# First steps of a two-transform and cosine-MLP kernel reordered: weight fold, cosine product and weight sums

## The chip, the cores and the metric

The kernel runs on one core of one Trainium2 chip. The metric is the device time of one execution in microseconds (us); lower is better. In the profile the engines are PE (TensorE; PEld is its weight load), DVE (VectorE), ACT (ScalarE), POOL (GpSimd) and SP (SyncE, which issues the DMAs).

## The reference

```python
X = np.fft.fft(x, axis=1)          # x: (8, 3008, 256) float32
X = np.fft.fft(X, axis=2)
a = X.real.reshape(8 * 3008, 256)
h = a @ w_in                       # w_in: (256, 2048)
g = h * np.cos(h)
out = g @ w_out                    # w_out: (2048, 256)
```

## The kernel before

The transform along the sequence is split 64 x 47. For each of the eight batches `first_half` does the part of length 47, its result goes through DRAM (`store_z`, `load_z`), and `second_half` does the part of length 64, group by group: six groups of token columns, 225 of them in group 0 and 256 in the others. It leaves a cosine part and a sine part per group in `pq`. The transform along the 256 channels is folded into the first weight matrix: `fold_weights(e, n)` multiplies a quarter n of `w_in` (512 columns) by the cosine (e = 0, into `WC`) or sine matrix (e = 1, into `WS`), and ACT copies the product out of PSUM. `take_wn(n)` then takes row 0 of that quarter of `WS` into the per-partition column `wn` with eight tiny matmuls and clears the row on GpSimd.

Because the output of a real transform has a mirrored half, one cosine product C and one sine product S give two token columns: C + S for a token and C - S for its mirror. That is one *half step* of the main loop, `k` = 0, 1, 2, ...; two half steps (u = 0, 1, two blocks of 128 hidden columns) are a *step* t = k // 2, and eight steps (fp = 0 to 7) finish one group of one batch. There are 384 steps. A half step h goes through:

- `seed` (ACT, L433): writes a start value into the PSUM tile `h.H`, a bank of four with tag "H";
- `mm1(h, 0)` (PE, L452, weights `WC`): adds the cosine product;
- `act_e` (ACT, L464): copies twice the cosine product to `ew`;
- `mm1(h, 1)` (PE, L452, weights `WS`): adds the sine product to the same bank, so it has to wait for `act_e`;
- `dve_h` (DVE, L468): `ew` minus `H`, the mirrored half;
- one half step later `act_round` (ACT, L480), `dve_frac` (DVE, L484) and `act_sin` (ACT, L490), which make the cosine;
- two half steps later `dve_g` (DVE, L494), the product h cos h;
- after both halves of a step `sums` (GpSimd, L510, L516, L517) makes four sums of the blocks;
- three steps later (`LAG`) `mm2` (PE, L543), the second matrix product. It works on seven products instead of eight: four with `g` blocks, of which the fourth needs the sums already, and three more with the sums. For the seven it needs sums of the output weights: `combine_w2(f0, f1)` (L418) makes them out of `w2` into `VX`, four instructions for two values of fp, each 128 x 256, reading `w2` with a step of two elements.

The schedule is written out by hand: instructions are queued per engine in the order of the program, each engine works its queue in order, and semaphores carry the dependencies. So what stands ahead of an instruction on its own engine decides as much as its data. In half step k the order around the change is: `mm1(k, 0)`, `act_e(k)`, `mm2` products 0 to 2 or 4 to 6, `dve_g(k-2)` (and `sums`), `act_round(k-1)`, `seed(k+1)`, `dve_frac(k-1)`, `act_sin(k-1)`, `mm1(k, 1)`, `mm2` product 3, `dve_h(k)`; then, after an odd k, the extra calls of the table `opening` for step t, and then those of `todo` (the next batch's transform).

Before the loop the first quarters are folded while the first x loads arrive; the last quarter's sine fold is queued in k = 0, its cosine fold and `take_wn(3)` after k = 1, and the four calls of `combine_w2` after t = 0, 1, 5 and 6, on DVE. `w2` comes in four DMAs of 512 KB: two issued at 35.9 to 36.9 us and two at 48.4 to 51.4 us.

Of the kernel before, what the change touches and what calls it, by code (L numbers as in the profile page):

```python
# [25 lines left out]
XP = 2 * IP  # L26
NG = 6
LAG = 3
SIN_SCALE = -float(np.float32(6.283185005187988))


# [50 lines left out]
def _width(g):  # L82
    return 225 if g == 0 else 256
# [24 lines left out]
def kernel(  # L108
# [7 lines left out]
    nc = tc.nc  # L116
# [78 lines left out]
    WC = cpool.tile([128, NDFF], FP, tag="WC", name="WC")  # L195
    WS = cpool.tile([128, NDFF], FP, tag="WS", name="WS")
# [4 lines left out]
    def psum(name, tag="H"):  # L201
        return ppool.tile([128, 512], FP, tag=tag, bufs=bank[tag], name=name)
# [85 lines left out]
    def second_half(b, g):  # L288

        T = _width(g)  # L290
        z2 = z2s[b]
        pb = psum("pb")
        for q in range(4):
            jj = 4 * g + q
            nc.tensor.matmul(  # L295
                pb[:, 128 * q : 128 * q + 128],
                lhsT=z2[:, jj * 128 : jj * 128 + 128],
                rhs=BJ[:, jj * 128 : jj * 128 + 128],
                start=q == 0,
                stop=True,  # L300
                skip_group_check=True,
            )
        pq = spool.tile([128, 512], FP, tag="pq", bufs=8, name="pq")
        pv = pq[:, 0 : 2 * T].rearrange("d (e t) -> d e t", e=2)
        bv = pb.rearrange("d (q e k) -> d e q k", q=4, e=2)
        if g == 0:
            nc.scalar.copy(
                out=pv[:, :, 0:192].rearrange("d e (q k) -> d e q k", k=64), in_=bv[:, :, 1:4, :]
            )
            nc.scalar.copy(out=pv[:, :, 192:225], in_=bv[:, :, 0, 0:33])  # L310
        else:
            nc.scalar.copy(out=pv.rearrange("d e (q k) -> d e q k", k=64), in_=bv)
        nb = spool.tile([128, 256], FP, tag="nb", bufs=8, name="nb")
        ready[b, g] = (pq, nb)
        if b == 0 and g == 0:
            return
        nd = dpool.tile([1, 256], FP, tag="nd", bufs=4, name="nd")
        nc.sync.dma_start(out=nd[:, 0:T], in_=pq[0:1, T : 2 * T])
        nc.sync.dma_start(out=nb[:, 0:T], in_=nd[0:1, 0:T].to_broadcast([128, T]))
# [9 lines left out]
    def transform(b):  # L329
        todo = {}  # L330

        def at(o, *call):
            todo.setdefault(o, []).append(call)

        for p in range(4):
            at(8 * p, load_x, b, p)
            for c, o, f in ((2 * p, 6, 9), (2 * p + 1, 9, 12)):
                at(8 * p + o, fold, b, c, 0)
                at(8 * p + o + 1, fold, b, c, 1)
                at(8 * p + f, first_half, b, c)  # L340
                at(8 * p + f + 1, store_z, b, c)
        at(23, load_z, b, 0)
        at(39, load_z, b, 1)
        for g in range(NG):
            at(42 + g, second_half, b, g)
        return todo
# [1 line left out]


    def fold_weights(e, n, tag="M"):  # L350
        W = WS if e else WC
        pw = psum("pw", tag)
        for i in range(2):
            nc.tensor.matmul(  # L354
                pw,
                lhsT=CS[i][:, 128 * e : 128 * e + 128],
                rhs=wr[n // 2][i][:, 512 * (n % 2) : 512 * (n % 2) + 512],
                start=(i == 0),
                stop=(i == 1),
            )  # L360
        nc.scalar.copy(out=W[:, 512 * n : 512 * n + 512], in_=pw)

    def take_wn(n):
        row = WS[0:1, 512 * n : 512 * n + 512]
        pw = psum("pw", "M")
        for k in range(4):
            nc.tensor.matmul(  # L367
                pw[:, k : k + 1],
                lhsT=row[:, 128 * k : 128 * k + 128],
                rhs=ones[:, 0:1],  # L370
                start=True,
                stop=True,
            )
        nc.scalar.copy(out=wn[:, 4 * n : 4 * n + 4], in_=pw[:, 0:4])
        if n == 0:
            nc.scalar.copy(out=wrow, in_=row[:, 0:256])
        nc.gpsimd.memset(row, 0.0)
# [15 lines left out]
    scratch = cpool.tile([1, 128], FP, tag="scratch", name="scratch")  # L393
    nc.scalar.activation(out=scratch, in_=ones, func=AF.Sin, bias=0.0, scale=SIN_SCALE / 8)

# [11 lines left out]
    vx = VX.rearrange("p (v f c) -> p v f c", v=4, c=128)  # L407
    wv = w2.rearrange("p (f u c j) -> p u j f c", u=2, j=2, c=128)

    def combine_w2(f0, f1):  # L410
        add, sub = ALU.add, ALU.subtract
        for dst, a, b, op in (
            (vx[:, 0], wv[:, 0, 1], wv[:, 0, 0], sub),
            (vx[:, 1], wv[:, 0, 1], wv[:, 1, 1], add),
            (vx[:, 2], vx[:, 0], wv[:, 1, 1], add),
            (vx[:, 3], wv[:, 1, 0], vx[:, 2], sub),
        ):
            nc.vector.tensor_tensor(  # L418
                out=dst[:, f0:f1], in0=a[:, f0:f1], in1=b[:, f0:f1], op=op
            )  # L420

# [15 lines left out]
    def seed_first(h):  # L437
        s, T = h.s, h.s.T
        nc.tensor.matmul(
            h.H[:, 0:T],  # L440
            lhsT=wrow[:, 128 * h.u : 128 * h.u + 128],
            rhs=s.pq[0:1, T : 2 * T],
            start=False,
            stop=True,
            skip_group_check=True,
        )

    def mm1(h, e):
        s, T = h.s, h.s.T
        W = WS if e else WC  # L450
        f = 2 * s.fp + h.u
        nc.tensor.matmul(  # L452
            h.H[:, 0:T],
            lhsT=W[:, 128 * f : 128 * f + 128],
            rhs=s.pq[:, e * T : e * T + T],
            start=False,
            stop=True,
            skip_group_check=True,
        )

    def act_e(h):
        T = h.s.T
        h.ew = spool.tile([128, 256], FP, tag="ew", bufs=2, name="ew")
        nc.scalar.mul(out=h.ew[:, 0:T], in_=h.H[:, 0:T], mul=2.0)  # L464
# [7 lines left out]
    def sides(h):  # L472
        T = h.s.T
        return h.s.r[:, 2 * T * h.u : 2 * T * h.u + 2 * T], h.H[:, 0 : 2 * T]
# [13 lines left out]
    def act_sin(h):  # L488
        r, _ = sides(h)
        nc.scalar.activation(out=r, in_=r, func=AF.Sin, bias=0.0, scale=SIN_SCALE)  # L490

# [216 lines left out]
    for half in range(2):  # L708
# [2 lines left out]
    load_w2(6, 8)  # L711
    load_bj(1024, NJ * 128)
    opening = {
        0: ((fold_weights, 0, 3), (take_wn, 3), (combine_w2, 0, 2)),
        1: ((combine_w2, 2, 4),),
        5: ((combine_w2, 4, 6), (second_half, 0, 1)),
        6: ((combine_w2, 6, 8),),
        10: ((second_half, 0, 2), (load_ident,)),
        14: ((second_half, 0, 3),),
        18: ((second_half, 0, 4),),  # L720
# [10 lines left out]
    n = len(steps)  # L731

    def step(t, last=None):
        s = steps[t] if 0 <= t < n else None
        return s if s is not None and (last is None or s.fp == 7) else None
# [3 lines left out]
    def unit(k):  # L739
        return halves[k] if 0 <= k < 2 * n else None  # L740
# [6 lines left out]
    steps[0].pq, steps[0].nb = ready[0, 0]  # L747
    for k in range(2 * (n + LAG)):
        t, u = divmod(k, 2)
        cur, prev, old, nxt = unit(k), unit(k - 1), unit(k - 2), unit(k + 1)  # L750
        done = step(t - LAG)
        full = step(t - LAG, True) if u else step(t - LAG - 1, True)
        if cur:
            if k % (2 * per) == 0:
                todo = transform(cur.s.b + 1) if cur.s.b + 1 < NB else {}
            mm1(cur, 0)
            if t == 0:
                seed_first(cur)
            act_e(cur)
            if k == 0:  # L760
                spread_nb()
                fold_weights(1, 3)
        if done:
            mm2(done, 4 * u, 4 * u + 3)
        if old:
            dve_g(old)
            if old.u:
                sums(old.s)
        if prev:
            act_round(prev)  # L770
        if nxt and k:
            seed(nxt)
        if full:
            take_m(full, 0 if u else 2, nc.scalar)
        if prev:
            dve_frac(prev)
            act_sin(prev)
        if cur:
            mm1(cur, 1)
        if done and u == 0:  # L780
            mm2(done, 3, 4)
        if cur:
            dve_h(cur)
        if full:
            take_m(full, 1 if u else 3, nc.vector)
        if u == 0:
            continue
        for i in range(6):
            s = step(t - LAG - 1 - i, True)
            if s:  # L790
                combine_m(s, i)
        for sg, lag in ((0, 5), (1, 7)):
            s = step(t - LAG - lag, True)
            if s:
                store_out(s, sg)
        for call in opening.pop(t, ()):
            call[0](*call[1:])
        for call in todo.pop(t % per, ()):
            call[0](*call[1:])
# [31 lines left out]
```

## Time and profile before

| | |
|---|---|
| time, median of 3 runs | 1979.02 us (1978.6 to 1979.23) |
| the profiled execution's own time | 1979.75 us |
| its span in the profile | 1977.9 us |
| PE, busy | 1960.2 us (99%) |
| DVE, ACT, POOL, busy | 1467.6 (74%), 1505.2 (76%), 1388.3 us (70%) |
| mean granted PE clock | 0.996 of full speed |
| first instruction of the main loop (`mm1(0, 0)`) | 38.6 us |

The profiled execution's time is 1.85 us longer than its span: what lies around the program's own instructions. All times below count from the start of the span. A PE row's duration holds the pipeline's fill; back to back, a product of `mm1` or `mm2` with 225 columns follows the one before after 0.38 us at the full clock and 0.75 us at half of it.

### The profile page before, as it was taken

Reading aid. Unit: us, or ns where it says so; the run is one execution under the profiler, and the core shown is the slowest. Engines: PE = TensorE matmul, PEld = TensorE weight load, DVE = VectorE, ACT = ScalarE, POOL = GpSimd, SP = SyncE. Lnnn points to the kernel's source line nnn. Section 1 sums busy time; section 2 is a strip of 40 time slices with the busy share of each in tenths; the row PEclk is TensorE's granted clock in tenths of the full one; section 3 lists DMA queues with packets and bytes.
Section 4 is the critical chain, followed back from the end, with each engine's and each line's share of the span. In section 5 each row is a group of like instructions: output and inputs, shape, how many; then the busy total and the mean of one; then the engine's idle time right before and its main releaser. Section 6 shows DMA issues by size and latency. Waiting matters only on the chain.

```text
span 1977.9 us, 29797 instructions
## 1 busy us (share of the span) xinstructions
PE 1960.2 (99%) x9360; PEld 1688.2 (85%) x9360; DVE 1467.6 (74%) x2540; ACT 1505.2 (76%) x3360; POOL 1388.3 (70%) x1577
## 2 busy tenths in 40 slices
PE   8899999999999999999999999999999999999998
PEld 4788889888998889888898888988889888898887
DVE  3777777777787777777777777777777777778776
ACT  3677778777787777777777777777777777778775
POOL 1577767777677776777667776687767777666775
PEclk9899999999999999999999999999999999999999
DMA  8422112120221212113121121113111231100001
GB/s 192 95 45 56 23 41 59 35 55 20 48 52 37 51 34 53 37 34 57 40 43 35 38 55 40 40 38 61 36 39 35 55 59 24 38 22 16 11 16 29
DMA packets 176691, 88.72 MB, mean 45 GB/s; under 512 B 103303, under 2 KB 173622, under 8 KB 174902
## 3 DMA queue, kind: packets, MB, share of 16 engines
q1 hardware_dynamic: 176374, 86.68, 21.2%
q8 instruction: 76, 1.25, 0.3%
q14 instruction: 81, 0.66, 0.1%
q10 hardware_dynamic: 160, 0.13, 0.0%
HBM read 49.50 MB, written 37.27 MB: 44 GB/s over the span
## 4 chain that ended last, share of the span: by engine, by line
PE 97%; DMA 1%; DVE 1%; SPq 0%; ACT 0%; issue 0%; POOL 0%; DVEq 0%; POOLq 0%
PE M L543 57%; PE H L452 33%; PE pz L242 3%; PE pb L295 2%; DMA xp<-in_x_dram 1%; DVE VX L418 0%; PE pw L354 0%; SPq L650 0%; DMA wr<-in_moe_w_in_dram 0%; DMA out_dram<-ob 0%; DVE r L484 0%; PE pd L399 0%; PE pw L367 0%; ACT ew L464 0%; ACT r L490 0%
## 5 line engine op out<-in xcount | busy, mean ns | idle before, releaser
L510 POOL TENSOR_TENSOR S<-r 128x512 f32<-128x512 f32 (+1 forms) x383 | 475.2, 1241 | 476.3 <-PE M L543 239.5
L484 DVE SCALAR_TENSOR_TENSOR r<-r,H 128x512 f32<-128x512 f32 (+1 forms) x768 | 518.9, 676 | 287.4 <-ACT r L480 273.5
L490 ACT ACTIVATE r<-r 128x512 f32<-128x512 f32 (+1 forms) x768 | 477.8, 622 | 277.2 <-DVE r L484 276.6
L543 PE MATMUL M<-S,VX 128*128 128x256 f32 (+1 forms) x2304 | 612.4, 375 | 0.0
L494 DVE SCALAR_TENSOR_TENSOR r<-H,r 128x512 f32<-128x512 f32 (+1 forms) x768 | 518.4, 675 | 99.7 <-ACT r L490 50.1
L543 PEld LDWEIGHTS M<-S,VX 128*128 128x128 f32 x2304 | 438.1, 190 | 50.3
L452 PE MATMUL H<-pq,WC 128*128 128x256 f32 (+1 forms) x1536 | 458.8, 380 | 0.4 <-ACT H L433 0.2
L452 PE MATMUL H<-pq,WS 128*128 128x256 f32 (+1 forms) x1536 | 452.8, 377 | 5.6 <-ACT ew L464 5.5
L480 ACT ACTIVATE r<-H 128x512 f32<-128x512 f32 (+1 forms) x768 | 447.7, 583 | 0.0
L468 DVE TENSOR_TENSOR H<-ew,H 128x256 f32<-128x256 f32 (+1 forms) x768 | 325.2, 423 | 95.4 <-PE H L452 22.1
L543 PE MATMUL M<-r,w 128*128 128x256 f32 (+1 forms) x1536 | 389.4, 376 | 0.0
L464 ACT ACTIVATE ew<-H 128x256 f32<-128x256 f32 (+1 forms) x768 | 290.3, 378 | 103.9 <-PE H L452 92.8
L433 ACT ACTIVATE H<-nb,wn 128x256 f32<-128x256 f32 (+1 forms) x766 | 366.0, 478 | 0.0
L452 PEld LDWEIGHTS H<-pq,WC 128*128 128x128 f32 x1536 | 280.1, 190 | 78.3 <-ACT r L490 43.6
L452 PEld LDWEIGHTS H<-pq,WS 128*128 128x128 f32 x1536 | 291.8, 190 | 40.2 <-ACT ew L464 8.6
L543 PEld LDWEIGHTS M<-r,w 128*128 128x128 f32 x1536 | 299.7, 197 | 29.4 <-ACT mr L566 1.2
L516 POOL TENSOR_TENSOR S<-S,r 128x256 f32<-128x256 f32 (+1 forms) x383 | 276.0, 721 | 30.0
L517 POOL TENSOR_TENSOR S<-r,S 128x256 f32<-128x256 f32 (+1 forms) x383 | 275.7, 720 | 30.0
L543 PE MATMUL M<-r,VX 128*128 128x256 f32 (+1 forms) x768 | 228.5, 379 | 0.2
L543 PE MATMUL M<-S,w 128*128 128x256 f32 (+1 forms) x768 | 225.2, 375 | 0.0
L543 PEld LDWEIGHTS M<-r,VX 128*128 128x128 f32 x768 | 143.3, 190 | 23.4 <-issue 7.6
L543 PEld LDWEIGHTS M<-S,w 128*128 128x128 f32 x768 | 150.5, 196 | 14.6
(67 smaller groups left out, 917.5 us busy)
## 6 DMA issues: line engine op xcount, KB each, us to landing
out_dram<-ob SPq DMA_DIRECT2D x728, 32.0 KB
xp<-in_x_dram SPq DMA_DIRECT2D x56, 256.0 KB
zd<-zs SPq DMA_DIRECT2D x112, 96.0 KB
z<-zd SPq DMA_DIRECT2D x28, 384.0 KB
xp<-in_x_dram SPq DMA_DIRECT2D x56, 120.0 KB
nb<-nd SPq DMA_DIRECT2D x40, 128.0 KB
wr<-in_moe_w_in_dram SPq DMA_DIRECT2D x8, 256.0 KB
w<-in_moe_w_out_dram SPq DMA_DIRECT2D x4, 512.0 KB
```

The source lines that it names most:

```text
L433: nc.scalar.activation(out=h.H[:, 0:T], in_=s.nb[:, 0:T], func=AF.Copy, bias=0.25, scale=wn[:, f : f + 1])
L452: nc.tensor.matmul(h.H[:, 0:T], lhsT=W[:, 128 * f : 128 * f + 128], rhs=s.pq[:, e * T : e * T + T], start=False, stop=True, skip_group_che ...
L464: nc.scalar.mul(out=h.ew[:, 0:T], in_=h.H[:, 0:T], mul=2.0)
L468: nc.vector.tensor_tensor(out=h.H[:, T : 2 * T][:, ::-1], in0=h.ew[:, 0:T], in1=h.H[:, 0:T], op=ALU.subtract)
L480: nc.scalar.activation(out=r, in_=y, func=AF.Copy, bias=BIG, scale=1.0)
L484: nc.vector.scalar_tensor_tensor(out=r, in0=r, scalar=-BIG, in1=y, op0=ALU.add, op1=ALU.subtract)
L490: nc.scalar.activation(out=r, in_=r, func=AF.Sin, bias=0.0, scale=SIN_SCALE)
L494: nc.vector.scalar_tensor_tensor(out=r, in0=y, scalar=-0.25, in1=r, op0=ALU.add, op1=ALU.mult)
L510: tt(out=sv[:, 0:2], in0=qv[:, 1:2].to_broadcast([128, 2, T]), in1=qv[:, 0:4:3], op=ALU.subtract,)
L516: tt(out=sv[:, 2], in0=sv[:, 1], in1=gv[:, 0, 0], op=ALU.subtract)
L517: tt(out=sv[:, 3], in0=gv[:, 1, 0], in1=sv[:, 2], op=ALU.add)
L543: nc.tensor.matmul(acc[key][m // 2][:, 256 * (m % 2) : 256 * (m % 2) + T], lhsT=w, rhs=a, start=first, stop=s.fp == 7, skip_group_check=True,)
```

## The change

Four things in the first twelve half steps:

- The first `second_half(0, 0)` takes its PSUM bank from the four with tag "M" instead of those with tag "H".
- The last quarter's cosine fold and `take_wn(3)` are cut in two. The matmuls of the fold go into k = 1 between `mm1(1, 0)` and `mm1(1, 1)`, those of `take_wn` into k = 2 between `mm1(2, 0)` and `mm1(2, 1)`; their copies on ACT follow `act_sin`.
- For half steps 3, 4 and 5 `mm1(h, 0)` and `act_e(h)` are queued one half step ahead: in half step h - 1, after `act_sin` and before `mm1(h - 1, 1)`.
- `combine_w2` runs on GpSimd instead of DVE. The calls for fp 0 to 3 both stand after t = 0, the other two are halved and stand after t = 3 and 4, and after t = 5 and 6.

```diff
+AHEAD = 2 * LAG
...
-        pb = psum("pb")
+        pb = psum("pb", "H" if b or g else "M")
...
     def fold_weights(e, n, tag="M"):
-        W = WS if e else WC
+        keep_weights(e, n, weights(e, n, tag))
+
+    def weights(e, n, tag="M"):
         pw = psum("pw", tag)
...
+        return pw
+
+    def keep_weights(e, n, pw):
+        W = WS if e else WC
         nc.scalar.copy(out=W[:, 512 * n : 512 * n + 512], in_=pw)
 
     def take_wn(n):
+        keep_wn(n, weight_row(n))
+
+    def weight_row(n):
         row = WS[0:1, 512 * n : 512 * n + 512]
         pw = psum("pw", "M")
...
+        return pw
+
+    def keep_wn(n, pw):
+        row = WS[0:1, 512 * n : 512 * n + 512]
         nc.scalar.copy(out=wn[:, 4 * n : 4 * n + 4], in_=pw[:, 0:4])
...
-    def combine_w2(f0, f1):
+    def combine_w2(f0, f1, k0=0, k1=4):
...
-        ):
-            nc.vector.tensor_tensor(
+        )[k0:k1]:
+            nc.gpsimd.tensor_tensor(
...
     opening = {
-        0: ((fold_weights, 0, 3), (take_wn, 3), (combine_w2, 0, 2)),
-        1: ((combine_w2, 2, 4),),
-        5: ((combine_w2, 4, 6), (second_half, 0, 1)),
-        6: ((combine_w2, 6, 8),),
+        0: ((combine_w2, 0, 2), (combine_w2, 2, 4)),
+        3: ((combine_w2, 4, 6, 0, 2),),
+        4: ((combine_w2, 4, 6, 2, 4),),
+        5: ((combine_w2, 6, 8, 0, 2), (second_half, 0, 1)),
+        6: ((combine_w2, 6, 8, 2, 4),),
...
-            mm1(cur, 0)
-            if t == 0:
-                seed_first(cur)
-            act_e(cur)
+            if k not in range(3, AHEAD):
+                mm1(cur, 0)
+                if t == 0:
+                    seed_first(cur)
+                act_e(cur)
             if k == 0:
                 spread_nb()
                 fold_weights(1, 3)
+            elif k == 1:
+                pw = weights(0, 3)
+            elif k == 2:
+                pw = weight_row(3)
...
             dve_frac(prev)
             act_sin(prev)
+        if k == 1:
+            keep_weights(0, 3, pw)
+        elif k == 2:
+            keep_wn(3, pw)
+        if k + 1 in range(3, AHEAD):
+            mm1(nxt, 0)
+            act_e(nxt)
         if cur:
             mm1(cur, 1)
```

## The prediction

> **What bounds the kernel now.** The page comes first.
>
> ```profile
> PE 1960.2 (99%) x9360; PEld 1688.2 (85%) x9360; DVE 1467.6 (74%) x2540; ACT 1505.2 (76%) x3360; POOL 1388.3 (70%) x1577
> ```
>
> PE is busy for all but 18 us, and from 88 us on every stretch I asked for is full. The change touches nothing behind half step 15, so it can win only what PE loses ahead of 88 us. The windows view, cut where the granted clock changes, shows where that is (window, PE, PEld, DVE, ACT, POOL busy, granted clock, DMA share, GB/s):
>
> ```profile
> 47.00:50.40 3.40, 2.29 (x9) 1.23 (x10) 1.62 (x4) 2.39 (x7) 0.52 (x1) 1.00 1.18 202
> 50.40:53.80 3.40, 2.95 (x7) 1.59 (x7) 3.31 (x7) 2.23 (x6) 2.51 (x3) 0.50 1.23 188
> 53.80:57.20 3.40, 1.81 (x5) 0.92 (x5) 2.89 (x7) 1.72 (x5) 0.75 (x1) 0.50 1.12 294
> 57.20:60.70 3.50, 3.50 (x11) 3.13 (x11) 1.62 (x3) 2.18 (x5) 1.65 (x3) 0.50 1.08 384
> 60.70:76.30 15.60, 15.60 (x85) 14.99 (x83) 12.34 (x24) 10.81 (x26) 7.27 (x9) 1.00 0.25 45
> 81.10:84.60 3.50, 1.35 (x6) 0.76 (x5) 3.10 (x7) 1.85 (x5) 0.79 (x1) 0.99 0.09 16
> 84.60:88.00 3.40, 3.40 (x10) 2.91 (x10) 1.31 (x3) 2.14 (x6) 2.83 (x4) 0.50 0.01 2
> ```
>
> There are two holes, 47 to 57 us and 81 to 84.6 us, and each brings a stretch at half clock (10.3 and 3.4 us) in which PE is full but slow. What made the holes is in the chain that ended last (start us, us, what):
>
> ```profile
> 49.88 0.25 ACT ew L464
> 50.13 0.44 ACT r L480
> 50.60 0.62 DVE r L484
> 51.23 0.31 DVE H L468
> 51.54 2.05 DVE VX L418 x3
> 53.61 0.43 DVE VX L418
> 54.04 0.54 DVE r L494
> ...
> 77.81 2.12 DVE VX L418 x3
> 79.96 1.37 DVE VX L418
> 81.33 0.54 DVE r L494
> ```
>
> The output weight sums (L418) stand in DVE's queue ahead of `dve_g` and `dve_frac`; `act_sin` waits for `dve_frac`, the next `act_e` stands behind `act_sin`, and `mm1(k, 1)` waits for `act_e`. The third look is DVE's and GpSimd's own timeline: one sum takes DVE 0.42 us where GpSimd is idle, but up to 1.37 us beside a GpSimd instruction.
>
> ```profile
> 46.25 0.42 DVE L418 TENSOR_TENSOR VX<-w,VX 128x256 f32<-128x256 f32 x1
> 79.61 1.44 POOL L218 TENSOR_TENSOR xf<-xp 94x508 f32<-94x508 f32 x1
> 79.96 1.37 DVE L418 TENSOR_TENSOR VX<-w,VX 128x256 f32<-128x256 f32 x1
> ```
>
> **What the holes cost.** Back to back, a product with 225 columns comes every 0.38 us at full clock (0.43 with 256). From `mm1(2, 0)` at 47.14 to `mm1(8, 0)` at 62.98 us lie 12 products of `mm1` and 10 of `mm2`, 22 x 0.38 = 8.4 us of work in 15.8. From `mm1(13, 0)` at 74.64 to `mm1(17, 0)` at 88.28 lie 20 products of 0.38 and two of 0.43, 8.5 us in 13.6. So 7.4 us are lost in the first hole, 5.2 in the second; the first can't vanish, since half steps 2 to 5 have no `mm2` beside them.
>
> **The sums on GpSimd.** 16 instructions leave DVE: 1.5 us at 45 us, 2.5 at 51.5, 2.4 at 72 and 3.5 at 77.7. On GpSimd the nearest row is L516, 128 x 256 out of SBUF: 0.73 us, one every 0.80. It has no operand with a step of two elements. From below the fold's subtraction (L218, one operand reversed, 94 x 508 in 1.26) gives 0.65 per 256 columns; from above 128 x 512 (1.28 us) stands for reading twice the words. I take 0.80, since the reversed operand costs nothing there. The first eight run as soon as `w2` lands: its 1 KB packets pass between 38 and 42 us, and the second half, issued from 48.4 us, between 53.8 and 57.5. So GpSimd, idle until 47.3 in the old trace, works on them from about 40.5 to 46.9. Queued behind them are the clearing of the `WS` row (0.52 us) and `sums(0)`, which can't start before about 49 anyway. The other eight go into steps 3 to 6, two in each: `sums` takes 2.65 us from start to free (1.14 + 2 x 0.75), plus 1.6, so 4.25 of a step of 11 x 0.38 = 4.2. In step 6 the next batch's fold (1.3) comes on top, and GpSimd falls 1.6 us behind. Who waits for that: `mm2` needs `sums` of a step about two steps after they can begin, 8.4 us less 1.1 for L510, so 7.3 us of cover; `VX` for fp 4 is ready about 66 us and used about 71. Cost: nothing. With p for one instruction, the cover goes in the opening at 40.5 + 8p + 1.1 = 56.4 (p = 1.85) and in steps 3 to 6 at 8p - 4.8 = 7.3 (p = 1.5).
>
> The Trainium skill speaks against this move (GPSIMD Engine Reference, section Engine selection): elementwise work belongs on VectorE, and two-input operations run about twice as slow on GpSimd. The trace agrees on the instruction alone, 0.73 against 0.42 us, but not for DVE's rows beside GpSimd, 0.65 to 1.37. By the rule 16 x 0.3 = 5 us would be lost if GpSimd's queue were on the path, which I deny.
>
> With DVE free, the second hole has no cause left: DVE has 0.54 + 0.39 + 0.54 = 1.5 us per half step, ACT's ring (below) 1.95, PE 2.1. **Gain 5.2 us**, its half clock included, since without a hole nothing lowers the clock.
>
> **Fold and row in the gaps.** In k = 1 the four fold passes (4 x 0.43, with their start 1.82) begin behind `seed_first` at 43.26 instead of 44.35, where PE used to wait 0.45 for `act_e`. `mm1(1, 1)` comes at 45.08 (before 43.87), `mm1(2, 0)` at 45.46 (before 47.14). The row's eight matmuls (0.95) follow until 46.85. On ACT the fold's copy (0.59) goes ahead of `act_e(2)`: 45.42, then 46.04. `seed(3)` at 46.72 no longer waits for `dve_g(0)`, because the first `pb` has left the H banks; that edit costs nothing and moves no DMA. SP's queue keeps its order.
>
> **The cosine product ahead.** Queued so, PE runs `mm1(k+1, 0)` before `mm1(k, 1)`, and `mm1(k+1, 0)` needs `seed(k+1)`, which on ACT stands behind `act_round(k-1)`. The ring from one `act_round` to the next is then: 0.43 to `seed`'s start, 0.50 for it, 0.38 for the first product, 0.69 until the second is out, 0.43 for `dve_h` and the handover, 2.43 us. The old order has two rings of 1.95: ACT's own (round 48.08, sin 49.31, next `act_e` 49.79, next round 50.03) and `act_e` to `act_e` over PE (47.82 to 49.79). So this part is slower by 0.48 per turn wherever nothing else interferes. Laid out with the old rows' durations: `act_round(2)` 48.71, `act_round(3)` 51.13, `act_round(4)` 53.55, `seed(6)` ends 54.44, `mm1(6, 0)` 54.48 (before 56.93). From there `mm2` fills PE: 11 products later `mm1(8, 0)` stands at 54.48 + 4.18 = 58.66 instead of 62.98. Gain 4.3 us at full clock.
>
> **The clock.** From 46.85 to 54.48 PE has 7 products, 2.7 us of work in 7.6, thinner than the window 47.0 to 50.4 after which the old trace falls to half clock. I therefore expect the fall at 50 to 52 us. A turn of the ring then takes 2.43 + 0.37 + 0.47 = 3.27; one to two turns are hit (1.05 on average), and the dense part begins about 55.5 at half clock. It returned, in both old cases, at the end of a full stretch of 3.4 us; so I count 2 to 4.4 us of dense work at half speed, of which half is lost, 1.6. First hole: 4.3 - 2.65 = **1.7 us**, between 0.5 and 4.3.
>
> The Trainium skill says the same of the gate (TensorE: Matmul & The Clock Gate, section What's actually happening): half rate after an idle window of about 3.4 us, full rate after a busy one. The rows 10.3 and 3.4 agree; how thin "idle" is they leave open, hence the next rival.
>
> **Sum.** 5.2 + 1.7 = 6.9 us: 1979.75 becomes 1972.85 for the profiled execution. The median lies 0.7 below that one, so 1972.1. A measurement of this kernel tells about 0.2%, 4 us, from no change: below 1975.1 counts as faster.
>
> **Rivals.**
>
> *The clock stays full.* If 35% of work is enough to hold it, both holes close as far as they can: 4.3 + 5.2 = 9.5 us, 1969.5. Against it: 47.0 to 50.4. Chance 0.12.
>
> *The second hole only moves.* If GpSimd's 1.6 us behind in step 6 reach PE after all (a late `xf`, S or `VX`), PE loses perhaps 2 us once and half of 3.4 at half clock, 3.7 of the 5.2: a gain of 3.2, 1975.8. Against it: 7.3 us of cover. Chance 0.14.
>
> *Slower: GpSimd reads the step of two badly.* It decides from p = 1.5 us and undoes the whole gain at p = 2.1 (8 x 0.6 = 4.8 in steps 3 to 6, 2.0 in the opening). At p = 2.5, twice the row of 128 x 512, the opening's sums end 5.2 us too late and the others 7.9 us: 13.1 against 6.9, 1985.3. For it: no row with that step on GpSimd. Against: the reversed operand is free. Chance 0.06.
>
> *The parts cancel.* The longer ring and three windows at half clock eat the first gain, and DVE's sums had hidden another wait of like size at 81 us: 1979. Against it: the chain names L418 directly. Chance 0.06.
>
> The forecast, the first hole at half clock and the second gone, keeps 0.62 (1971.4 to 1973.3).
>
> **How the numbers follow.** Faster: 0.62 + 0.12 + a part (0.05) of the second rival, 0.79. Same: 0.09 of it and 0.05 of the cancelling, 0.14. Slower: 0.07. The range takes in the full clock (1969.5, less 0.5 of spread between runs) and the moved hole: 1969.0 to 1976.0.
>
> **What would show it.** L418 on POOL at 0.7 to 0.8 us, the first eight over by 48 us; `mm1(2, 0)` about 45.5, `mm1(6, 0)` between 54.5 and 56; `act_round` to `act_round` 2.4 us or more for half steps 2 to 4; a clock of 0.5 from 50 to 52 us to 57 to 61; no PE gap over 0.5 us from there to 100 us. The prediction is wrong if L418 takes over 1.5 us, if PE waits on POOL, or if a hole is left at 70 to 85 us.

## The result and the profile after

The changed kernel took 1971.87 us (median of six runs, 1970.68 to 1973.18) against 1979.09 for the kernel before (six runs, 1978.60 to 1979.66): a ratio of 0.9963, 95% interval 0.9951 to 0.9976, so 7.2 us faster. The profiled execution took 1971.01 us with a span of 1969.2, 8.7 us shorter than before. L numbers of the changed kernel are its own: `combine_w2` is L432, `mm1` L466, `act_e` L478, `act_round` L494, `mm2` L557.

The page's busy times first:

```profile
PE 1954.4 (99%) x9360; PEld 1686.3 (86%) x9360; DVE 1458.7 (74%) x2524; ACT 1505.5 (76%) x3360; POOL 1398.8 (71%) x1593
```

16 instructions went from DVE to POOL, which is 10.5 us busier. PE's busy time fell by 5.8 us at the same number of products: it spent 10.2 us less at half clock (table below), and half of that, 5.1 us, is most of the fall. The windows view (window, PE, PEld, DVE, ACT, POOL busy, granted clock, DMA share, GB/s), cut at this run's clock changes:

```profile
46.80:50.20 3.40, 1.69 (x8) 0.99 (x6) 1.81 (x4) 2.54 (x7) 1.64 (x3) 1.00 1.17 201
50.20:53.60 3.40, 1.68 (x6) 0.98 (x6) 2.42 (x6) 2.50 (x6) 0.99 (x3) 1.00 1.22 190
53.60:57.00 3.40, 3.25 (x9) 2.94 (x10) 1.97 (x4) 2.40 (x6) 2.18 (x3) 0.50 1.15 346
57.00:60.50 3.50, 3.50 (x20) 3.44 (x19) 2.03 (x5) 1.84 (x5) 1.78 (x3) 1.00 1.00 308
60.50:76.30 15.80, 15.80 (x88) 15.51 (x87) 11.72 (x22) 12.40 (x30) 13.11 (x18) 1.00 0.45 76
76.30:80.00 3.70, 3.70 (x21) 3.49 (x20) 2.93 (x6) 3.05 (x9) 3.54 (x5) 1.00 0.42 65
80.00:88.00 8.00, 8.00 (x46) 6.70 (x45) 5.96 (x11) 6.07 (x14) 6.14 (x8) 1.00 0.01 2
```

The second hole is gone: PE is full from 57 us on. The first is still there, 47 to 53.6 us, with PE half empty, but only one stretch of 3.4 us at half clock follows. What fills it is no longer DVE's output weight sums; in the chain that ended last (start us, us, what) it is the ring over the seed (L447):

```profile
47.50 0.41 DVE H L482
47.91 0.02 issue
47.93 0.55 ACT r L494
48.48 0.35 ACT H L447
48.83 0.04 issue
48.87 1.04 PE H L466 x4
49.92 0.02 issue
49.94 0.41 DVE H L482
50.35 0.02 issue
50.37 0.55 ACT r L494
```

From one `act_round` to the next: 50.37 - 47.93 = 2.44 us. GpSimd's timeline shows the eight opening sums and how `sums(0)` (L524) follows without having waited for them. They start when the first half of `w2` is there: the first row waits for several semaphores, and the wait that this trace puts down to PE is put down to the DMA of `w2` in the run "sums twice".

```profile
40.52 1.42 POOL L432 TENSOR_TENSOR VX<-w 128x256 f32<-128x256 f32 x2 [5.65 <-PE pw L357]
41.89 0.73 POOL L432 TENSOR_TENSOR VX<-VX,w 128x256 f32<-128x256 f32 x1
...
45.58 0.74 POOL L432 TENSOR_TENSOR VX<-w,VX 128x256 f32<-128x256 f32 x1
46.31 0.52 POOL L391 MEMSET WS<- 1x512 f32 x1
48.51 1.07 POOL L524 TENSOR_TENSOR S<-r 128x450 f32<-128x450 f32 x1 [1.68 <-DVE r L508]
```

To compare runs, the starts of `mm1(k, 0)` on PE are counted from `mm1(0, 0)`; that one itself stood between 36.8 and 38.6 us in the runs, as the first loads came (38.57 before, 37.69 after; of this 0.9 us, 0.77 is the last x load in the chain, which ended at 26.67 us before and at 25.90 after, ahead of anything that the change touches). So 0.9 of the 8.7 us between the two spans is not counted as the change's.

| us after mm1(0, 0) | mm1(2, 0) | mm1(6, 0) | mm1(8, 0) | mm1(17, 0) | half clock, us | median, us |
|---|---|---|---|---|---|---|
| before | 8.57 | 18.36 | 24.41 | 49.71 | 10.24 + 3.41 | 1979.09 |
| changed | 6.98 | 16.06 | 21.95 | 42.09 | 3.41 | 1971.87 |
| changed, again | 6.98 | 16.06 | 21.73 | 41.87 | 3.41 | 1972.03 |
| sums only | 8.57 | 17.55 | 23.34 | 43.48 | 10.24 | 1971.14 |
| all but sums | 6.98 | 18.50 | 24.50 | 49.80 | 10.24 + 3.41 | 1978.80 |
| not ahead | 6.98 | 15.30 | 20.79 | 40.93 | 6.83 | 1969.38 |
| sums thrice | 6.97 | 17.38 | 25.48 | 50.54 | 10.24 + 3.41 | 1983.44 |
| sums twice | 6.98 | 17.74 | 23.48 | 43.63 | 10.24 | 1972.53 |
| fold back | 8.57 | 19.95 | 26.45 | 46.59 | 13.65 | 1974.93 |
| seed early | 6.98 | 14.48 | 18.73 | 38.81 | none | 1969.41 |
| PE filled | 6.98 | 16.16 | 20.35 | 40.49 | none | 1970.00 |
| seed early and filled | 6.98 | 14.48 | 18.73 | 38.80 | none | 1967.72 |
| not ahead and filled | 6.98 | 14.66 | 18.96 | 39.09 | none | 1968.03 |

The half-clock column counts the stretches before 100 us of the profiled execution, which is one run; the medians are of 5 to 11 runs. The kernel before ran at 1978.45, 1978.64 and 1978.74 us beside the three sets of experiments, so medians of different sets are best compared by what each gained on the kernel before beside it: the changed kernel 7.2 and, run again, 6.7 us.

### The profile page after: what moved, and what is told of

It reads as the page before. It is cut to its first block, busy times and chain, and to the rows that moved or that the text cites. A ratio compares the mean times of both kernels' runs of the same rounds, so it can differ in the third digit from the quotient of the medians.

```text
span 1969.2 us, 29797 instructions
## 1 busy us (share of the span) xinstructions
PE 1954.4 (99%) x9360; PEld 1686.3 (86%) x9360; DVE 1458.7 (74%) x2524; ACT 1505.5 (76%) x3360; POOL 1398.8 (71%) x1593
## 4 chain that ended last, share of the span: by engine, by line
PE 97%; DMA 1%; SPq 0%; ACT 0%; DVE 0%; issue 0%; POOL 0%; DVEq 0%; POOLq 0%
PE M L557 58%; PE H L466 34%; PE pz L243 3%; PE pb L296 2%; DMA xp<-in_x_dram 1%; PE pw L357 0%; SPq L664 0%; DMA wr<-in_moe_w_in_dram 0%; DMA out_dram<-ob 0%; PE pd L413 0%; ACT r L494 0%; ACT H L447 0%; DVE H L482 0%; PE H L453 0%; PE pw L377 0%
## 5 line engine op out<-in xcount | busy, mean ns | idle before, releaser
L524 POOL TENSOR_TENSOR S<-r 128x512 f32<-128x512 f32 (+1 forms) x383 | 475.1, 1240 | 463.5 <-PE M L557 237.7
L557 PE MATMUL M<-S,VX 128*128 128x256 f32 (+1 forms) x2304 | 612.4, 375 | 0.0
L557 PEld LDWEIGHTS M<-S,VX 128*128 128x128 f32 x2304 | 437.7, 190 | 50.1
L466 PE MATMUL H<-pq,WC 128*128 128x256 f32 (+1 forms) x1536 | 457.7, 380 | 3.7 <-ACT H L447 3.7
L466 PE MATMUL H<-pq,WS 128*128 128x256 f32 (+1 forms) x1536 | 450.2, 375 | 0.1
L494 ACT ACTIVATE r<-H 128x512 f32<-128x512 f32 (+1 forms) x768 | 447.7, 583 | 1.1 <-DVE H L482 1.1
L557 PE MATMUL M<-r,w 128*128 128x256 f32 (+1 forms) x1536 | 388.7, 375 | 0.0
L478 ACT ACTIVATE ew<-H 128x256 f32<-128x256 f32 (+1 forms) x768 | 290.4, 378 | 101.7 <-PE H L466 90.3
L447 ACT ACTIVATE H<-nb,wn 128x256 f32<-128x256 f32 (+1 forms) x766 | 366.0, 478 | 0.0
L466 PEld LDWEIGHTS H<-pq,WC 128*128 128x128 f32 x1536 | 279.8, 190 | 80.5 <-ACT r L504 43.6
L557 PEld LDWEIGHTS M<-r,w 128*128 128x128 f32 x1536 | 299.2, 197 | 29.3 <-ACT mr L580 1.2
L466 PEld LDWEIGHTS H<-pq,WS 128*128 128x128 f32 x1536 | 291.5, 190 | 32.6 <-issue 0.7
L557 PE MATMUL M<-r,VX 128*128 128x256 f32 (+1 forms) x768 | 228.1, 378 | 0.2
L557 PE MATMUL M<-S,w 128*128 128x256 f32 (+1 forms) x768 | 225.2, 375 | 0.0
L557 PEld LDWEIGHTS M<-r,VX 128*128 128x128 f32 x768 | 143.0, 190 | 23.4 <-issue 7.7
L557 PEld LDWEIGHTS M<-S,w 128*128 128x128 f32 x768 | 150.4, 196 | 14.6
```

The source lines that it names most:

```text
L447: nc.scalar.activation(out=h.H[:, 0:T], in_=s.nb[:, 0:T], func=AF.Copy, bias=0.25, scale=wn[:, f : f + 1])
L466: nc.tensor.matmul(h.H[:, 0:T], lhsT=W[:, 128 * f : 128 * f + 128], rhs=s.pq[:, e * T : e * T + T], start=False, stop=True, skip_group_che ...
L494: nc.scalar.activation(out=r, in_=y, func=AF.Copy, bias=BIG, scale=1.0)
L524: tt(out=sv[:, 0:2], in0=qv[:, 1:2].to_broadcast([128, 2, T]), in1=qv[:, 0:4:3], op=ALU.subtract,)
L557: nc.tensor.matmul(acc[key][m // 2][:, 256 * (m % 2) : 256 * (m % 2) + T], lhsT=w, rhs=a, start=first, stop=s.fp == 7, skip_group_check=True,)
```

## The experiments

Theory A was the prediction's: DVE's output weight sums made both holes, the cosine product ahead makes a longer ring, the clock takes the rest. Theory B: the reordering of fold and cosine product carries the gain.

**Sums only.** The kernel before, with `combine_w2` on GpSimd as in the change and its calls at the new places:

```diff
-            nc.vector.tensor_tensor(
+            nc.gpsimd.tensor_tensor(
...
-        0: ((fold_weights, 0, 3), (take_wn, 3), (combine_w2, 0, 2)),
-        1: ((combine_w2, 2, 4),),
+        0: ((fold_weights, 0, 3), (take_wn, 3), (combine_w2, 0, 2), (combine_w2, 2, 4)),
+        3: ((combine_w2, 4, 6, 0, 2),),
...
```

> The kernel before with one part of the change: combine_w2 on GpSimd at its new places, everything else as before. Theory A (the output weight sums in DVE's queue made both holes): the second hole, 13.6 us from mm1(13, 0) to mm1(17, 0), falls to 8.5 (5.2 gained); in the first hole the 2.5 us stall goes but the ring of 1.95 to 2.33 us per half step stays, so mm1(6, 0) comes 1.3 us earlier; together 6.5, 1972.6 us. Theory B (the reordering of fold and cosine product carries the gain): 1976 us or more.

1971.14 us, ratio 0.9964 (0.9952 to 0.9977): as fast as the whole change. From `mm1(8, 0)` to `mm1(17, 0)` it needs 43.48 - 23.34 = 20.14 us, before 25.30, the changed kernel 20.14: the second hole is the sums' alone, 5.16 us. In the first hole `mm1(6, 0)` came 0.8 earlier, not 1.3, and `mm1(8, 0)` 1.07, so there the sums were a small part; its profiled run was the slowest of five (1972.9). The run moves the sums to another engine and to other places in the order at once. Sums left on DVE at the new places were not run, so how much the engine and how much the places are worth is open.

**All but sums.** The changed kernel with `combine_w2` on DVE after t = 0, 1, 5 and 6 again (the same lines the other way).

> The changed kernel with combine_w2 back on DVE, after t = 0, 1, 5 and 6 as before; the other edits stay. Theory A: the hole at about 81 us comes back with its 3.4 us of half clock, and the DVE stall of 2.5 us in the first; only 0.5 to 1.5 us are left of the gain, 1977.6 to 1978.6 us. Theory B: 1974 us or less.

1978.80 us, ratio 1.0000 (0.9992 to 1.0009): nothing is left, a little less than the 0.5 to 1.5 us that A gave it. The chain of this kernel has the sums (L432) in both places again, now also in the first half steps:

```profile
45.42 1.01 DVE VX L432 x3
...
51.99 1.01 DVE VX L432 x3
...
77.17 2.12 DVE VX L432 x3
79.30 0.02 issue
79.32 1.37 DVE VX L432
```

The fold's 1.6 us at `mm1(2, 0)` were used up by half step 6. Theory B falls with these two.

**Not ahead.** The changed kernel without cosine products ahead:

```diff
-AHEAD = 2 * LAG
+AHEAD = 3
```

> The changed kernel with AHEAD = 3, so no cosine product is queued ahead; the rest stays. Theory A (queued ahead, the ring over seed, both products and dve_h takes 2.43 us per turn where the old order has 1.95): three turns are 0.48 shorter each, mm1(6, 0) comes 1.4 us earlier after the loop's start, 1970.5 us. Theory B (the cosine product ahead hides act_e and helps): 1 us or more slower than the changed kernel, 1973 us.

1969.38 us (1967.38 to 1969.74), a gain of 9.1 us on the kernel before beside it, about 2 more than the changed kernel's, although its profiled run had twice its time at half clock. The chain now alternates ACT and DVE, with no PE product and no seed in it until the clock falls:

```profile
45.45 0.44 ACT r L494
45.89 0.02 issue
45.91 0.63 DVE r L498
46.55 0.02 issue
46.57 0.58 ACT r L504
47.15 0.05 ACT wn L388
47.20 0.26 ACT ew L478
47.46 0.44 ACT r L494
```

45.45 to 47.46 is a turn of 2.0 us against 2.44, and `mm1(6, 0)` comes 0.76 us earlier: queuing the product ahead costs time. Of the 2 us between the medians the rest is not traced: `mm1(17, 0)` of the two profiled runs differs by 1.16.

**Seed early.** If the ring of 2.44 us runs over the seed, an earlier seed opens it:

```diff
-        if nxt and k:
-            seed(nxt)
+        for j in {1: (2, 3), 2: (4,), 3: (5,), 4: (6,), 5: ()}.get(k, (k + 1,)):
+            if k and unit(j):
+                seed(unit(j))
```

> The changed kernel, with seed(3) to seed(6) queued one half step earlier on ACT (seed(2) and seed(3) both in k = 1), so that the cosine product ahead doesn't wait for a seed behind act_round. Theory A (the ring of 2.43 us runs over the seed): mm1(3, 0) to mm1(6, 0) come 1.95 apart, mm1(6, 0) 14.6 us after mm1(0, 0) instead of 16.06; about 1970.4 us. Rival (something else makes the turn 2.4 us, dve_h or DVE's order): mm1(6, 0) stays at 16 us and the time at 1971.9.

1969.41 us, `mm1(6, 0)` at 14.48: the seed it was. The products of half steps 3 to 5 came even closer together than 1.95 (1.45, 0.87 and 1.66): in PE's timeline those of 3 and 4 waited for nothing, that of 5 only 0.33 us for its seed. The ring itself turns on ACT and DVE, with no seed in its chain.

**PE filled.** The changed kernel with spare products in the waits:

```diff
         if cur:
             mm1(cur, 1)
+        if k in (2, 3, 4):
+            keep_busy(3, "M", 256)
```

> The changed kernel with three spare products of 256 columns (1.28 us, their result unused) behind mm1(k, 1) in k = 2, 3 and 4, where PE waits 1.4 us for the seed. Theory A (thin work on PE lowers its clock, and that costs half of the stretch): no stretch at half clock after 45 us, mm1(6, 0) unmoved at 16.1 us after mm1(0, 0), mm1(8, 0) at 20.3 instead of 21.95; 1970 us, and runs closer together. Rival (the spare products only stand in the way): mm1(6, 0) later and 1972.5 us or more.

1970.00 us (1969.15 to 1970.05). No half clock, `mm1(6, 0)` where it was (16.16) and `mm1(8, 0)` at 20.35: the 1.6 us between the kernels are the clock's. The five runs lie within 0.9 us, all at a mean clock of 0.999 or 1.000; those of the changed kernel within 2.5 and, in its second set, 4.4 us, at 0.996 to 0.999.

```profile
46.00:50.00 4.00, 3.64 (x21) 3.04 (x21) 2.57 (x5) 2.99 (x9) 2.17 (x4) 1.00 1.15 233
50.00:54.00 4.00, 3.89 (x19) 3.24 (x18) 2.49 (x6) 2.90 (x8) 1.52 (x4) 1.00 1.22 186
54.00:58.00 4.00, 4.00 (x23) 3.88 (x22) 3.28 (x6) 3.17 (x9) 2.47 (x4) 1.00 1.11 342
```

**Seed early and filled, not ahead and filled.** Two versions meant to beat both kernels: the seeds early with `keep_busy(2, "M", 256)` at the same place, and `AHEAD = 3` with one `keep_busy(1, "M", 384)` between the two products of half steps 3 to 5.

> Both at once: seeds one half step earlier and two spare products of 256 columns behind mm1(k, 1) in k = 2, 3 and 4. Theory A: mm1(6, 0) at 14.6 and mm1(8, 0) at 18.8 us after mm1(0, 0), the clock full; 1968.8 us. Rival (PE's work is still too thin): half clock for 3.4 us or more, 1970.5 us.

> No cosine product ahead, and one spare product of 384 columns between mm1(k, 0) and mm1(k, 1) in k = 3, 4 and 5, in the time PE waits for act_e. Theory A: the ring of 1.95 us holds and the clock stays full, so mm1(6, 0) comes at 14.8 and mm1(8, 0) at 18.9 us after mm1(0, 0) (15.3 and 20.8 without the filling, at half clock for 6.8 us); 1967.5 us against 1969.4. Rival (still too thin): half clock again, 1969.4 us.

1967.72 (1967.00 to 1969.16) and 1968.03 us (1967.21 to 1969.28), both without half clock before 100 us; `mm1(6, 0)` at 14.48 and 14.66, `mm1(8, 0)` at 18.73 and 18.96, as expected. With ratios of 0.9947 (0.9935 to 0.9960) and 0.9948 (0.9936 to 0.9961) they have the lowest medians here, 10.9 and 10.6 us below the kernel before. They can't be told apart, and their intervals overlap with those of the seed early alone (0.9955, 0.9943 to 0.9968) and of not ahead (0.9951, 0.9939 to 0.9964).

**Sums thrice, sums twice.** How much cover do GpSimd's sums have? Each instruction was issued three times, and in the other run two times (`range(2)`):

```diff
+            for _ in range(3):
-            nc.gpsimd.tensor_tensor(
+                nc.gpsimd.tensor_tensor(
```

> The changed kernel with each combine_w2 instruction issued three times (same result), so one sum costs GpSimd 2.4 us. Theory A (GpSimd's sums are hidden, with cover up to 1.85 us in the opening and 1.5 us in steps 3 to 6): cover is exceeded, 8 x 2.4 pushes sums(0) 3.5 us past mm2's need, and steps 3 to 6 fall about 7 us behind it, with half clock on top: 1980 to 1986 us. Rival (much more slack on GpSimd than counted): within 1 us of the changed kernel, 1972 to 1973 us. Rival (sums on the path already): 8 x 1.6 + 8 x 1.6 = 25 us more.

> The changed kernel with each combine_w2 instruction issued twice (same result), 1.6 us per sum on GpSimd. Theory A (cover up to 1.85 us in the opening, 1.5 in steps 3 to 6): sums(0) still comes in time, steps 3 to 6 miss by at most 0.7 us; 1972 to 1973 us, so GpSimd could take twice as long without loss. Rival (GpSimd's sums are already at the edge): 3 us or more slower than the changed kernel.

Three times: 1983.44 us (1982.18 to 1984.77), slower than the kernel before (ratio 1.0027, 1.0016 to 1.0037). `mm1(7, 0)` came at 23.57 instead of 20.04 us, 3.5 late, and between `mm1(8, 0)` and `mm1(17, 0)` another 4.9 were lost. PE waits for GpSimd at both places that the prediction named, in its own timeline:

```profile
60.61 0.65 PE L558 MATMUL M<-S,VX 128*128 128x225 f32 x2 [1.60 <-POOL S L525]
79.03 0.65 PE L558 MATMUL M<-r,VX 128*128 128x225 f32 x2 [1.16 <-POOL VX L433]
```

Twice: 1972.53 us, the changed kernel run beside it 1972.03. PE waits for GpSimd nowhere in its trace from 38 to 100 us; that `mm1(6, 0)` is late there goes with three stretches at half clock, from 48.5 us. Within the spread of the runs, twice the work on GpSimd is free, three times is not.

**Fold back.** The changed kernel with the cosine fold and `take_wn(3)` whole behind k = 1 again:

```diff
-            elif k == 1:
-                pw = weights(0, 3)
-            elif k == 2:
-                pw = weight_row(3)
...
-        0: ((combine_w2, 0, 2), (combine_w2, 2, 4)),
+        0: ((fold_weights, 0, 3), (take_wn, 3), (combine_w2, 0, 2), (combine_w2, 2, 4)),
```

> The changed kernel with the last quarter's cosine fold and take_wn(3) whole again behind k = 1, ahead of the sums; cosine products ahead and sums on GpSimd stay. Theory A (the cut fold gains 1.6 us at mm1(2, 0), and nothing later takes it back): mm1(2, 0) at 8.6 instead of 6.98 us after mm1(0, 0), mm1(6, 0) at 17.6 instead of 16.06, 1973.5 us. Rival (the early start is eaten by the next wait): mm1(6, 0) at 16.1 and 1971.9 us.

1974.93 us (eleven runs, 1974.16 to 1977.23), 2.9 slower than the changed kernel beside it, not 1.6. `mm1(2, 0)` was 1.6 late as expected, `mm1(6, 0)` 3.9: the profiled run fell to half clock at 48.4 us, four stretches of 3.41 long, and the ring's turns became 16.67 - 13.39 = 3.28 us:

```profile
50.98 1.12 PE L466 MATMUL H<-pq,WC 128*128 128x225 f32 x2 [1.41 <-ACT H L447]
51.90 0.96 PE L466 MATMUL H<-pq,WS 128*128 128x225 f32 x2
54.26 1.12 PE L466 MATMUL H<-pq,WC 128*128 128x225 f32 x2 [1.41 <-ACT H L447]
```

The prediction had worked out 3.27 for a turn at half clock.

**The changed kernel again.**

> The changed kernel itself once more, as the measure for the two others of this chip. Theory A (the clock's half-speed stretches start at chance within the thin part of PE's work): 1970.7 to 1973.2 us again, spread by some 2 us, longer where the mean clock is lower.

1972.03 us (1969.18 to 1973.54). The run at a mean clock of 0.999 took 1969.18, the others, at 0.996 to 0.998, 1970.6 to 1973.5. So one of the changed kernel's twelve runs came close to the time of the full clock without any filling.

## Why the prediction was right

It forecast 1972.1 us and 6.9 gained; 1971.87 and 7.2 were measured. By its steps:

- *The sums on GpSimd, hidden.* Right: the median rows of its three forms are 0.73 to 0.74 us, with the step of two elements, where 0.73 (0.80 apart) was assumed; the first eight were over at 46.3 us (46.9), the others ran at 61, 66, 70 and 75 us, and no instruction waited for L432. The cover was sized well: 1.6 us per sum is free, 2.4 is not, and the prediction had put the limits at 1.85 in the opening and 1.5 in steps 3 to 6. So the rival "GpSimd reads the step of two badly" has its mechanism confirmed and its threshold bracketed, and only its premise was wrong.
- *The second hole, 5.2 us.* Measured 5.16, in the changed kernel and with the sums alone. It did not move elsewhere.
- *Fold and row in the gaps.* `mm1(2, 0)` 6.98 us after `mm1(0, 0)`, worked out 6.89. Its worth was put at the 1.6 us shift alone; taken out it costs 2.9. The profiled run with the later start was at half clock for 13.65 us against 3.41; that this is the reason in the other runs too is likely, not shown.
- *The ring of 2.43 us.* Measured 2.44, `mm1(6, 0)` at 16.06 (15.91). That the cosine product ahead is a loss was stated as 0.48 us a turn; taking it out gains about 2 us, more than the 1.4 expected.
- *The clock.* This term was mis-sized: two to three stretches at half clock from 50 to 52 us on, costing 2.65, left 1.7 us to the first hole. Both profiled runs of the changed kernel had one, later than forecast, from 53.6 and 53.0 us, and ended it at 57.0 and 56.4. The first gained 24.41 - 21.95 = 2.46, and the stretch cost it 21.95 - 16.06 - 4.18 = 1.7. Judged by the medians, filling PE gained 1.4 us (against the kernel before beside each) to 1.9 (directly), also less than the 2.65. The full-clock rival, 1969.5, came true in one run of twelve; it takes the filling to have it in all.
- *The parts.* They do not add: sums alone 7.3 us, all the rest alone -0.3, all together 7.2. The fold's gain and the loss by the product ahead nearly cancel, and both are changed by where the half clock falls. That the forecast is met within 0.3 us is partly luck: the changed kernel's own runs spread over 1969.2 to 1973.5.

The Trainium skill's rule against GpSimd for two-input elementwise work (GPSIMD Engine Reference, section Engine selection) holds for the instruction, 0.73 against 0.42 us, and would have spoken against the one edit that brought the gain.

## What to carry to other kernels

An instruction is judged by the queue it stands in: work that takes 1.7 times as long on an engine with time to spare was free while its cover lasted, and the same work in the queue of a dependency ring cost 5.2 us in the second hole, of which half of the 3.4 us at half clock, 1.7, is an estimate of the clock's part. Before queuing a product ahead, follow the ring it then belongs to: here it made `mm1(k, 1)` wait for the next half step's seed. Where PE's work is thin, spare products in its waits kept the clock up, where they fitted the wait: all 15 runs of the three filled kernels had a mean clock of 0.999 or more.

## What was not expected of the hardware

The fall to half clock does not follow PE's busy share in the stretch before it. In the changed kernel 46.8 to 50.2 us, 1.69 of 3.40 busy, was followed by full clock, and the next such stretch, 1.68, by half; in the kernel without the product ahead 2.74 of 3.40 was followed by half clock at once:

```profile
45.20:48.60 3.40, 2.74 (x16) 1.99 (x15) 2.75 (x6) 2.70 (x9) 1.23 (x2) 1.00 1.23 210
48.60:52.00 3.40, 2.50 (x7) 1.08 (x5) 2.53 (x5) 2.76 (x7) 1.71 (x4) 0.50 1.23 188
```

Every half-clock stretch before 100 us was a multiple of 3.41 us (3.41, 6.83, 10.24, 13.65), as the Trainium skill's window says (TensorE: Matmul & The Clock Gate, section What's actually happening); what within a window decides was not settled here. Columns order it better than busy time: the 2.74 us hold most of the eight matmuls of `take_wn`, 1.05 us for eight columns. Cut the profiled runs between 40 and 96 us into windows of 3.41 us at the clock's changes, and count the columns of the matmul instructions that start in each window at full clock (two instructions of 225 or 256 make a product). Every window with 2149 or more was followed by full clock, all six with 1133 or less by half, and of the nine with 1350 to 1806 six by half.

With the seeds early and no filling, one run had a mean clock of 0.999 (the profiled one, at full clock up to 1962 us) and four 0.997 or 0.998: the same program took 1967.8 to 1970.9 us, the fastest at the highest clock.
